# Windowed attention with a gated feed-forward: loads one group less ahead, keys transposed behind x, the third group's weights transposed by DMA

## The chip, the core and the metric

The kernel runs on one core of one Trainium2 chip. The metric is the device time of one execution in microseconds (us). The profile is one execution, taken by the hardware profiler. Engines: PE is TensorE (its weight loads are listed as PEld), DVE VectorE, ACT ScalarE, POOL GpSimd, SP SyncE, which here only issues DMAs. Each engine works through its own instructions in the order in which they are written; an instruction that waits holds up all behind it on that engine. A DMA runs beside the engines once it is issued.

## The reference

Attention with four sink keys and a window of 128, on 4 batches, 8 heads, 768 positions, 64 columns a head; then a feed-forward block on the joined heads.

```python
scores = scale * np.matmul(q, k.transpose(0, 1, 3, 2))
keep = (pos[None, :] < n_sink) | ((rel >= 0) & (rel < window))
a = softmax(np.where(keep, scores, -1e9))
x = np.matmul(a, v)            # then (4 * 768) x 512, heads side by side
h = x @ w_in                   # 512 -> 2048
out = (h * sigmoid(1.702 * h)) @ w_out
```

## The kernel before

The 3072 positions are cut into 12 groups of 256 (`NG`, three to a batch), and a group into two blocks of 128. What happens to a group:

- **Loads** (`load_part`, line 123, issued by POOL, float32 to fp16 on the way): parts 0 and 1 are the queries' two blocks, 2 and 3 the keys', into `qkn`; 4 and 5 are the values', into `vn`. Each is 128 KB as fp16.
- **Transposition of queries and keys** into `qkT`: on PE with a copy by ACT or DVE for groups 0 to 3 (`qk_block`), by one DMA of 512 KB on SP's queue for groups from 4 on (`transposed_qk`, line 169).
- **Sinks** (`sinks`: PE and DVE; `sink_keys` first copies a batch's four sink keys out of `qkT`), **scores** of a head pair `hp` (0 to 3) into a PSUM tile `nat` with two buffers, **maxima** on DVE, **weights** (`weights`, line 255: four exponentials on ACT into `A`).
- **Weights transposed** into `AT` (`weights_transposed`): for groups 0 to 2 on PE into a PSUM bank (line 269) with a copy by ACT (271) or DVE (273), for the later ones by a DMA of 128 KB on SP's queue (line 275).
- **lower** (DVE, line 305) and **upper** (POOL, line 318) cut the two triangles out of `AT`, **values** (PE) multiplies them with `vn`, **normal** (DVE, lines 361 and 362) divides by the sums into `xn`.
- **x_transposed**: `xn` into `xT`, by a DMA of 256 KB on SP's queue for groups from 2 on (line 380).
- **hidden** (PE, line 394, then the gelu on ACT, line 397): eight tiles, `F2` 0 to 7, in two PSUM banks `mm`. **o** (`out_part`, line 409): the second matrix, two blocks of four parts, and `out_store` (a copy by ACT or DVE and a DMA on SP's queue).

The order is written out by hand. Lines 442 to 628 hold the start, in which groups 0 to 2 and the first pieces of the feed-forward are interleaved. Then follows the main loop. **Round n** has these parts for group n's attention, group n-1's hidden phase and group n-2's output:

1. `second(n, ...)`, for n over 2: weights of head pairs 0 and 1 and their transposition, the output matmuls of group n-2 with scores and maxima of pairs 2 and 3 in between, the two stores, weights and transpositions of pairs 2 and 3, `lower(n, 0)`, and at its end `transposed_qk(n + 2)`. In rounds 5 and 8, where group n+1 opens a batch, POOL copies that batch's sink keys first.
2. On POOL: `upper` of pairs 0 and 1, then the query and key loads of group n+3 with `upper` of pairs 2 and 3 between them.
3. The hidden phase: eight tiles of group n-1. At `F2` = 1 come sinks, scores and maxima of group n+1's pairs 0 and 1 (`ahead`) and `lower(n, 1)`; at `F2` = 3, 4, 6 and 7 the values and normalising of group n; `lower(n, 3)` stands ahead of the first normalising. The two value loads of group n+3 are paced by a small POOL copy of what `normal` wrote (`paced_load`).
4. `x_transposed(n)`.

On SP's queue a round is therefore: x of group n-1 (from the round before), AT pairs 0 and 1, a store, AT pair 2, a store, AT pair 3, queries and keys of group n+2.

Buffers: `qkn` 3, `qkT` 4, `A` 4, `AT` 6, `lo` and `up` 4 each, `xT` and `gT` 3.

Of the kernel before, what the change touches and what calls it, by code (L numbers as in the profile page):

```python
# [57 lines left out]
def kernel(  # L58
# [20 lines left out]
    NG = B * NT  # L79
# [31 lines left out]
    def load_part(g: int, part: int):  # L111


        b, t = divmod(g, NT)
        e, i = divmod(part, 2)
        rows = slice(t * TG + i * P, t * TG + (i + 1) * P)
        if part == 0:
            G[g]["qkn"] = work.tile([P, 4, DM], FP16, tag="qkn", bufs=3, name=f"qkn{g}")
        if part < 4:
            dst = G[g]["qkn"][:, part].rearrange("s (h d) -> s h d", h=H)  # L120
        else:
            dst = vn[b][t][:, i, :, 0:D]
        nc.gpsimd.dma_start(dst, (q, k, v)[e][b, :, rows].rearrange("h s d -> s h d"))  # L123

    def load_qk(g: int):
        for part in range(4):
            load_part(g, part)

    def load_v(g: int):
        for part in (4, 5):  # L130
            load_part(g, part)
# [35 lines left out]
    def transposed_qk(g: int):  # L167
        if g >= EARLY:
            nc.sync.dma_start_transpose(qk_tile(g), G[g]["qkn"].rearrange("p a c -> p (a c)"))
# [79 lines left out]
    def weights(g: int, hp: int):  # L249

        nat, bias = G[g]["nat", hp], G[g]["bias"]
        A = work.tile([P, 4, P], FP16, tag="A", bufs=4, name=f"A{g}_{hp}")
        for h in range(2):
            for i in range(2):
                nc.scalar.activation(  # L255
                    out=A[:, 2 * h + i], in_=nat[:, h, i, P:], func=AF.Exp, bias=bias[:, i, hp, h : h + 1],
                    scale=scale,
                )
        G[g]["A", hp] = A

    def weights_transposed(g: int, hp: int):
        A = G[g]["A", hp]
        AT = work.tile([P, 2, 2, P], FP16, tag="AT", bufs=6, name=f"AT{g}_{hp}")
        flat = AT.rearrange("p h i s -> p (h i) s")
        if g < 3:
            bank = av_bank if g == 2 or (g, hp) == (1, 3) else mm_bank
            tp = bank(f"tA{g}_{hp}", (P, 4, P), FP16)
            for a in range(4):
                nc.tensor.transpose(tp[:, a], A[:, a], ident)
            if g == 0 or hp < (2 if g == 2 else 3):  # L270
                nc.scalar.copy(flat, tp)
            else:
                nc.vector.tensor_copy(out=flat, in_=tp)
        else:
            nc.sync.dma_start_transpose(flat, A.rearrange("p a c -> p (a c)"))
        G[g]["AT", hp] = AT
# [10 lines left out]
    def sink_weights(g: int):  # L287
        ts_ = G[g]["ts"]
        As = sinkA[g % 2]
        nc.scalar.activation(out=As[:, 0:64], in_=ts_.rearrange("p a j -> p (a j)"), func=AF.Exp)  # L290
        G[g]["As"] = As
# [19 lines left out]
    def upper(g: int, hp: int):  # L311
        AT, i0 = G[g]["AT", hp], int(g % NT == 0)
        up = work.tile([P, 2, 2, P], FP16, tag="up", bufs=4, name=f"up{g}_{hp}")
        if i0:
            out, in_, rows = up[:, :, 1], AT[:, :, 1], 2
        else:
            out, in_, rows = up.rearrange("p h i s -> p (h i) s"), AT.rearrange("p h i s -> p (h i) s"), 4
        nc.gpsimd.affine_select(  # L318
            out=out, in_=in_, pattern=[[0, rows], [-1, P]], compare_op=ALU.is_gt, fill=zero_reg, base=0,
            channel_multiplier=1,  # L320
        )
        G[g]["up", hp] = up
# [26 lines left out]
    def paced_load(g: int, part: int, n: int, hp: int):  # L349

        if g < NG:
            nc.gpsimd.tensor_copy(out=pace, in_=G[n]["rcp", hp][0:1, 0, 0:1])
            load_part(g, part)
# [12 lines left out]
    def x_transposed(g: int):  # L366
        xT = work.tile([P, 2 * HP, P], FP16, tag="xT", bufs=3, name=f"xT{g}")
        xn = G[g]["xn"].rearrange("p i a h d -> p (i a h d)")
        if g < 2:
            bank = mm_bank if g == 0 else av_bank  # L370
            for i in range(2):
                tp = bank(f"tx{g}_{i}", (P, HP, P), FP16)
                for c in range(HP):
                    nc.tensor.transpose(tp[:, c], xn[:, (HP * i + c) * P : (HP * i + c + 1) * P], ident)
                if g == 0 or i == 0:
                    nc.scalar.copy(xT[:, bass.ts(i, HP)], tp)
                else:
                    nc.vector.tensor_copy(out=xT[:, bass.ts(i, HP)], in_=tp)
        else:
            nc.sync.dma_start_transpose(xT, xn)  # L380
        G[g]["xT"] = xT.rearrange("p (i c) s -> p i c s", i=2)
# [49 lines left out]
    def out_store(g: int, i: int):  # L431
        b, t = divmod(g, NT)
        osb = work.tile([P, DM], FP32, tag="osb", bufs=3, name=f"osb{g}_{i}")
        if i == 0:
            nc.scalar.copy(osb, G[g]["o", i])
        else:
            nc.vector.tensor_copy(out=osb, in_=G[g]["o", i])
        r = b * S + t * TG + i * P
        nc.sync.dma_start(out[r : r + P, :], osb)
# [54 lines left out]
    def o(g: int, i: int, *parts):  # L494
        if 0 <= g < NG:
            for p in parts:
                out_part(g, i, p)
# [75 lines left out]
    load_part(3, 3)  # L573
    load_v(2)
    load_v(3)
    load_qk(4)
    load_v(4)
    hidden(0, 1)
    sink_transposed(1)
    qk_block(2, 0, by_dve)  # L580
# [17 lines left out]

    for hp in (0, 1):
        weights(2, hp)  # L600
    o(0, 0, 0, 1)
    for a in (0, 1):
        qk_block(3, a, by_dve)
    o(0, 0, 2, 3)
    scores(2, 2)
    maxima(2, 2)
    weights_transposed(2, 0)
    upper(2, 0)
    o(0, 1, 0)
    out_store(0, 0)  # L610
    weights_transposed(2, 1)
    upper(2, 1)
    scores(2, 3)
    maxima(2, 3)
# [9 lines left out]
    lower(2, 0)  # L624
    o(0, 1, 3)
    weights(2, 3)
    sink_weights(2)
    out_store(0, 1)

    def second(n: int, g2: int, att: bool):  # L630

        if att and n + 1 < NG and (n + 1) % NT == 0:
            sink_keys((n + 1) // NT, nc.gpsimd.tensor_copy)
        if att:
            for hp in (0, 1):
                weights(n, hp)
                weights_transposed(n, hp)
        o(g2, 0, 0, 1, 2, 3)
        if att:
            scores(n, 2)  # L640
            maxima(n, 2)
        if g2 == NG - 1:
            out_store(g2, 0)
            out_last(g2, 1)
            return
        o(g2, 1, 0)
        if att:
            scores(n, 3)
            maxima(n, 3)
            sink_terms(n)  # L650
        o(g2, 1, 1, 2, 3)
        out_store(g2, 0)
        if att:
            weights(n, 2)
            weights_transposed(n, 2)
        out_store(g2, 1)
        if att:
            weights(n, 3)
            weights_transposed(n, 3)
            sink_weights(n)  # L660
            lower(n, 0)
            if n + 2 < NG:
                transposed_qk(n + 2)

    for n in range(2, NG + LAG2):
        att = n < NG
        g1, g2 = n - LAG1, n - LAG2

        if n > 2:
            second(n, g2, att)  # L670
        else:
            transposed_qk(n + 2)
        if att:
            if n > 2:
                upper(n, 0)
                upper(n, 1)
            for part in range(4):
                if n + 3 < NG:
                    load_part(n + 3, part)
                if n > 2 and part < 2:  # L680
                    upper(n, 2 + part)
        if n in (2, 3, 4):
            sink_columns(n - 1)

        for F2 in range(NF // 2):
            if 0 <= g1 < NG:
                hidden(g1, F2)
            if not att:
                continue
            if n == 2 and F2 == 0:  # L690
                weights_transposed(n, 3)
                upper(n, 3)
            if F2 == 1:
                sink_transposed(n)
                ahead(n + 1, 0)
                lower(n, 1)
                ahead(n + 1, 1)
            if F2 == 2:
                lower(n, 2)
            for hp, at in enumerate((3, 4, 6, 7) if n + 1 < NG else (4, 5, 6, 7)):  # L700
                if F2 == at:
                    values(n, hp)
                    if hp == 0:
                        lower(n, 3)
                    normal(n, hp)
                    if hp in (1, 2):
                        paced_load(n + 3, 3 + hp, n, hp)
        if att:
            x_transposed(n)
            if n + 1 < NG and (n + 1) % NT == 0:  # L710
                sink_values((n + 1) // NT)

# [33 lines left out]
```

## Time and profile before

| | |
|---|---|
| median of three runs | 243.81 us (243.29 to 244.23) |
| the profiled execution | 243.37 us |
| its span | 241.5 us |
| PE busy | 222.7 us, 92% of the span |
| ACT, DVE, POOL busy | 156.1, 146.1, 104.7 us |
| DMA packets' time on POOL's queue (q0), on SP's (q1) | 78.9% and 43.0% of 16 engines' span |
| mean granted clock of PE | 0.998 |

Times within the profile count from the span's start; the rest of the execution's time, 1.9 us, lies around it. "Busy" of PE is modelled, since matmuls overlap each other; a share near 100% in a stretch means that no idle time is seen there, not that PE is at its peak. The time that packets took counts every packet in flight on an engine, so that shares of the queues can add up to more than 100%.

### The profile page before, as it was taken

The page shows a single profiled execution, that of the slowest core. Times are in us where ns is not written, and L with a number is a line of the kernel's source. Part 1 is how long each engine was busy: PE and PEld are TensorE (multiplying, and loading weights), DVE is VectorE, ACT ScalarE, POOL GpSimd, SP SyncE. Part 2 cuts the span into 40 slices and gives each one's busy share as a digit, 9 for nine tenths or more (in the row PEclk, how much of TensorE's full clock was granted, in tenths as well). Part 3 has the DMA queues.
Part 4 walks back from the last instruction along what each step waited for, and adds up shares of the span by engine and source line. Part 5 has one row for each costly group of instructions (what it writes and reads, how often), then busy time and mean ns, then how long its engine had stood idle before and what let it go on. Part 6 is the DMA issues. An engine that isn't in the chain of part 4 may idle for free.

```text
span 241.5 us, 5809 instructions
## 1 busy us (share of the span) xinstructions
PE 222.7 (92%) x2220; PEld 155.7 (64%) x2220; DVE 146.1 (61%) x389; ACT 156.1 (65%) x355; POOL 104.7 (43%) x158
## 2 busy tenths in 40 slices
PE   1656799999999999999999999999999999999994
PEld 0443678569658569478478487486585685684863
DVE  4688856488568378377667575586682893830100
ACT  2268693784866875785786776677668658760531
POOL 8977486847326447354438057058020310310000
PEclk9999999999999999999999999999999999999999
DMA  8999999999999999999999999999982513503102
GB/s 74 151 188 193 177 207 180 154 120 145 127 150 190 138 165 157 112 189 121 124 183 159 153 163 141 173 134 139 129 214 46 151 25 62 148 11 87 46 0 87
DMA packets 130699, 32.07 MB, mean 133 GB/s; under 512 B 123120, under 2 KB 127728, under 8 KB 130672
## 3 DMA queue, kind: packets, MB, share of 16 engines
q0 software_dynamic: 79104, 13.64, 78.9%
q1 hardware_dynamic: 50992, 17.88, 43.0%
q8 instruction: 17, 0.28, 0.5%
q10 hardware_dynamic: 576, 0.20, 0.3%
q14 instruction: 10, 0.08, 0.1%
HBM read 27.50 MB, written 6.29 MB: 140 GB/s over the span
## 4 chain that ended last, share of the span: by engine, by line
PE 63%; DVE 14%; ACT 13%; DMA 5%; issue 3%; POOL 1%; SPq 0%; ACTq 0%; DVEq 0%; POOLq 0%
PE hT L394 28%; PE o L409 22%; ACT A L255 6%; DVE m L240 5%; DVE nat L236 5%; ACT L397 3%; PE nat L224 3%; DMA AT<-A 2%; PE av L344 2%; DMA qkn<-in_k_dram 2%; ACT gT L397 2%; PE av L332 2%; PE av L340 2%; PE o L420 1%; DVE xn L362 1%
## 5 line engine op out<-in xcount | busy, mean ns | idle before, releaser
L394 PE MATMUL hT<-xT,w_in 128*128 128x256 f16 x768 | 95.1, 274 | 1.1 <-ACT gT L397 0.4
L409 PE MATMUL o<-w_out,gT 128*128 128x512 f16 x368 | 85.4, 380 | 0.0
L397 ACT ACTIVATE gT<-hT 128x512 f16<-128x512 f32 x96 | 56.1, 597 | 41.2 <-PE hT L394 40.9
L394 PEld LDWEIGHTS <-w_in 128*128 128x128 f16 x768 | 72.7, 98 | 13.4 <-issue 0.6
L318 POOL TENSOR_SCALAR_AFFINE_SELECT up<-AT 128x512 f16<-128x512 f16 (+1 forms) x48 | 27.8, 585 | 99.1 <-DMA AT<-A 91.7
L255 ACT ACTIVATE A<-nat,bias 128x128 f16<-128x128 f32 x192 | 53.7, 376 | 18.6 <-DVE bias L244 17.1
L409 PEld LDWEIGHTS <-gT 128*128 128x128 f16 x368 | 33.6, 98 | 37.2
L236 DVE COPY_PREDICATED nat<-prev,nat 128x512 f32<-128x512 uint16 x48 | 33.2, 692 | 28.7 <-PE nat L224 19.0
L240 DVE TENSOR_REDUCE m<-nat 128x4 f32<-128x512 f32 x48 | 33.2, 691 | 1.7
L123 POOL DMA_DIRECT2D vn<-in_v_dram x24 | 21.3, 898 | 3.4 <-DMA w_out<-in_moe_w_out_dram 2.3
L123 POOL DMA_DIRECT2D qkn<-in_k_dram x24 | 21.3, 894 | 2.5 <-DMA w_in<-in_moe_w_in_dram 2.0
L123 POOL DMA_DIRECT2D qkn<-in_q_dram x24 | 21.6, 910 | 1.3 <-POOLq L727 0.8
L305 DVE TENSOR_TENSOR lo<-AT,own 128x512 f16<-128x512 f16 (+1 forms) x48 | 18.2, 397 | 5.9 <-DMA AT<-A 5.7
L362 DVE TENSOR_TENSOR xn<-av,rcp 128x256 f16<-128x256 f32 x48 | 20.4, 424 | 1.7
L340 PE MATMUL av<-vn,up 128*128 128x65 f16 x160 | 18.4, 196 | 0.0
L344 PE MATMUL av<-vn,lo 128*128 128x65 f16 x160 | 18.3, 196 | 0.0
L332 PE MATMUL av<-vs,AsT 128*128 128x130 f16 x80 | 16.5, 224 | 0.6 <-DVE xn L362 0.3
L224 PEld LDWEIGHTS <-qkT 64*128 64x128 f16 x352 | 11.8, 100 | 7.7 <-issue 7.0
L224 PE MATMUL nat<-qkT 64*128 64x128 f16 x288 | 16.6, 232 | 0.0
L361 DVE RECIPROCAL rcp<-av 128x4 f32<-128x4 f32 x48 | 8.5, 178 | 12.3 <-PE av L344 12.0
L340 PEld LDWEIGHTS <-up 128*128 128x128 f16 x160 | 14.8, 100 | 1.4 <-POOL up L318 0.5
L397 ACT ACT_TABLE_LOAD x11 | 14.1, 1283 | 0.2
(58 smaller groups left out, 180.3 us busy)
## 6 DMA issues: line engine op xcount, KB each, us to landing
out_dram<-osb SPq DMA_DIRECT2D x23, 256.0 KB
qkn<-in_q_dram POOLq DMA_DIRECT2D x24, 128.0 KB, 5.6
qkn<-in_k_dram POOLq DMA_DIRECT2D x24, 128.0 KB, 5.4
vn<-in_v_dram POOLq DMA_DIRECT2D x24, 128.0 KB, 6.6
w_in<-in_moe_w_in_dram POOLq DMA_DIRECT2D x4, 512.0 KB, 10.4
w_out<-in_moe_w_out_dram POOLq DMA_DIRECT2D x4, 512.0 KB, 11.6
AT<-A SPq DMA_TRANSPOSE x36
xT<-xn SPq DMA_TRANSPOSE x10
```

The costliest lines, as they stand in the source:

```text
L123: nc.gpsimd.dma_start(dst, (q, k, v)[e][b, :, rows].rearrange("h s d -> s h d"))
L224: nc.tensor.matmul(o, qkT[r, 0, i, hp], keys[r], start=True, stop=True)
L236: nc.vector.copy_predicated(out=nat[:, :, :, P:], mask=kinds(take_prev, g % NT), data=nat[:, :, :, 0:P])
L240: nc.vector.tensor_reduce(out=m1.rearrange("p h i -> p (h i)"), in_=nat.rearrange("p h i c -> p (h i) c")[:, :, P:], axis=AX.X, op=ALU.max,)
L255: nc.scalar.activation(out=A[:, 2 * h + i], in_=nat[:, h, i, P:], func=AF.Exp, bias=bias[:, i, hp, h : h + 1], scale=scale,)
L318: nc.gpsimd.affine_select(out=out, in_=in_, pattern=[[0, rows], [-1, P]], compare_op=ALU.is_gt, fill=zero_reg, base=0, channel_multiplier=1,)
L340: nc.tensor.matmul(av[:, i, h], up[:, h, i], vn[b][J // 2][:, J % 2, head], start=False, stop=False)
L344: nc.tensor.matmul(av[:, i, h], own_w[:, h, i], vn[b][t][:, i, head], start=(I == 0), stop=(I == 0 or h == 1))
L362: nc.vector.tensor_tensor(out=G[g]["xn"][:, :, hp], in0=av[:, :, :, 0:D], in1=rcp.to_broadcast((P, 2, 2, D)), op=ALU.mult)
L394: nc.tensor.matmul(hT[:, f], w_in16[:, c, bass.ts(F, P)], xT[:, :, c], start=(c == 0), stop=(c == 3))
L397: nc.scalar.activation(out=G[g]["gT"][:, 2 * F2 : 2 * F2 + 2].rearrange("p f s -> p (f s)"), in_=hT.rearrange("p f i s -> p (f i s)"), fun ...
L409: nc.tensor.matmul(o, gT[:, F, bass.ts(i, P)], w_out16[:, F], start=(F == 0), stop=(F == NF - 1))
```

## The change

- Groups are loaded one round less ahead: the start no longer loads group 4, and round n loads group n+2 instead of n+3, at the same places; so round 9 has loads too.
- `transposed_qk(n + 2)` moves from `second` (for n = 2: from the top of the loop) to the end of the round, behind `x_transposed(n)`. On SP's queue it then stands behind x of group n and ahead of the next round's four AT.
- Group 2's weights are transposed by DMA like the later groups', each right behind its weights; the upper triangle of its fourth pair is issued in the start, ahead of group 4's loads.

```diff
@@ weights_transposed
-        if g < 3:
-            bank = av_bank if g == 2 or (g, hp) == (1, 3) else mm_bank
+        if g < 2:
+            bank = av_bank if (g, hp) == (1, 3) else mm_bank
...
-            if g == 0 or hp < (2 if g == 2 else 3):
+            if g == 0 or hp < 3:
@@ the start
     load_v(2)
     load_v(3)
-    load_qk(4)
-    load_v(4)
...
     for hp in (0, 1):
         weights(2, hp)
+        weights_transposed(2, hp)
     o(0, 0, 0, 1)
...
-    weights_transposed(2, 0)
     upper(2, 0)
     o(0, 1, 0)
     out_store(0, 0)
-    weights_transposed(2, 1)
     upper(2, 1)
...
     weights(2, 3)
+    weights_transposed(2, 3)
     sink_weights(2)
     out_store(0, 1)
+    upper(2, 3)
@@ second
             lower(n, 0)
-            if n + 2 < NG:
-                transposed_qk(n + 2)
@@ the main loop
         if n > 2:
             second(n, g2, att)
-        else:
-            transposed_qk(n + 2)
...
-                if n + 3 < NG:
-                    load_part(n + 3, part)
+                if n + 2 < NG:
+                    load_part(n + 2, part)
...
-            if n == 2 and F2 == 0:
-                weights_transposed(n, 3)
-                upper(n, 3)
...
-                        paced_load(n + 3, 3 + hp, n, hp)
+                        paced_load(n + 2, 3 + hp, n, hp)
         if att:
             x_transposed(n)
+            if n + 2 < NG:
+                transposed_qk(n + 2)
```

## The prediction

> **What bounds the kernel now.** I read the page's busy shares and chain first, then the work by stage, one stage for each round of the main loop, cut where the round's hidden phase starts.
>
> ```profile
> PE 63%; DVE 14%; ACT 13%; DMA 5%; issue 3%; POOL 1%; SPq 0%; ACTq 0%; DVEq 0%; POOLq 0%
> ```
>
> ```profile
> 70.48:87.33 16.85, 16.74 (x166) 11.46 (x165) 10.54 (x29) 12.34 (x30) 7.09 (x13) 1.00 1.41 143
> 87.33:104.62 17.29, 17.21 (x179) 11.93 (x178) 11.08 (x29) 12.31 (x29) 9.43 (x16) 1.00 1.57 162
> 104.62:122.41 17.79, 17.37 (x178) 11.93 (x177) 12.58 (x30) 12.30 (x29) 8.87 (x12) 1.00 1.52 137
> 122.41:139.23 16.82, 16.74 (x166) 11.47 (x165) 10.54 (x29) 12.30 (x29) 7.28 (x13) 1.00 1.53 170
> 190.72:208.37 17.65, 17.21 (x178) 11.94 (x177) 11.80 (x30) 12.67 (x30) 2.55 (x4) 1.00 0.32 76
> ```
>
> After the stretch stand its length and the busy time of PE, PEld, DVE, ACT and POOL. PE is idle only 0.08 to 0.11 us of a round (length less PE's busy time), so TensorE is the bound. In the third of these rows, round 5, it is idle 0.42. The chain of waits says why: round 5's fourth weight transposition.
>
> ```profile
> 105.97 6.02 DMA AT<-A
> ...
> 112.02 0.04 DVE lo L305
> 112.05 0.31 issue
> 112.36 0.18 DVE rcp L361
> ```
>
> That transposition landed 7.37 us after the hidden phase began at 104.62 and cost 0.42 - 0.08 = 0.34 us. In round 8 it landed 6.97 after (the chip's completion count in the trace: 163.49 against 156.52) and cost nothing. So a fourth tile that lands later than about **7.0 us into the hidden phase** holds PE, microsecond for microsecond. Nothing in this kernel has much slack against its DMAs, and it is their order that the change moves.
>
> **Part one, on the path: the third group's weights leave PE.** PE's own rows in time order:
>
> ```profile
> 47.90 0.40 PE L269 MATMUL tA<-ident,A 128*128 128x128 f16 x4
> ...
> 49.00 0.39 PE L269 MATMUL tA<-ident,A 128*128 128x128 f16 x4
> ...
> 52.09 0.38 PE L269 MATMUL tA<-ident,A 128*128 128x128 f16 x4
> 52.31 1.03 PE L409 MATMUL o<-w_out,gT 128*128 128x512 f16 x4
> 53.17 1.04 PE L394 MATMUL hT<-xT,w_in 128*128 128x256 f16 x8
> 54.05 0.39 PE L269 MATMUL tA<-ident,A 128*128 128x128 f16 x4
> ```
>
> From each start to PE's next start: 0.23, 0.32, 0.22 and 0.22 us, with 0.25 of idle time ahead of the third (four output matmuls start at 50.97 and take 0.86). Together 1.24. Not all of it reaches the end: the second hidden tile needs the bank that VectorE empties. That copy runs at 53.38 to 54.07 and, with one AT copy gone before it, can end at 53.48 (the keys' copies end at 52.37, then 0.42 for a lower triangle, 0.69 for the copy). Then 0.87 for the tile and 0.88 for the sinks and scores: the third tile starts at 55.23 instead of 56.03. **Gain 0.8 us.** ScalarE loses two copies (0.58 each), but its chain to the first gelu waits for VectorE's maxima; gain nothing.
>
> In their place stand four DMA transpositions. Alone, one lands 2.4 us after its issue (round 9's and 10's rows). The first is issued when its weights are ready, about 46.9, among loads that fill the DMA until 48.45; VectorE wants it at 52.4. The last is ready about 52.6, lands about 55.1 and is wanted at 59.0. So all are hidden; if the loads held the first for over 5 us, the 0.8 would be gone. [...]
>
> **Part two: loads one group less ahead.** Group 4's six loads leave the start. They were the last there (issued 41.87 to 47.56), nothing else waits behind them, so the start gains nothing. They return in round 2 behind the fourth upper triangle, about 55.8 to 59.4, and land about 63; the transposition of group 4 then comes at 64. No stall there. Each later round loads as many bytes at the same places as before, and round 9, which had none, now loads group 11. But the keys now land just before they are needed.
>
> **Part three: the keys' transposition (qkT) goes from the end of SP's queue of a round to just behind x's.** This is SP's queue around round 5, its start and the time it held the queue:
>
> ```profile
> 97.71 1.23 SPq L380 DMA_TRANSPOSE xT<-xn  x1
> 99.80 2.54 SPq L275 DMA_TRANSPOSE AT<-A  x2
> 102.44 0.52 SPq L439 DMA_DIRECT2D out_dram<-osb  x1
> 103.90 1.19 SPq L275 DMA_TRANSPOSE AT<-A  x1
> 105.54 0.33 SPq L439 DMA_DIRECT2D out_dram<-osb  x1
> 105.97 1.22 SPq L275 DMA_TRANSPOSE AT<-A  x1
> 107.41 3.79 SPq L169 DMA_TRANSPOSE qkT<-qkn  x1
> ```
>
> Let X be x's issue (97.71). The hidden phase starts at X+6.9. Now qkT stands ahead of all four AT:
> - It starts when its last key load has landed: after X by 0.9, 1.7, 2.6, 2.1, 2.0, 2.8 us in rounds 3 to 8 of the trace (completion counts), mean X+2.0; not before X+1.3, when x's issue ends.
> - It holds SP for 3.5 us (mean of the seven issues beside other transfers, 2.86 to 4.01). The one of round 9, after the last load, took 1.77.
> - Two AT, a store, an AT, a store, back to back: 2.54 + 0.52 + 1.19 + 0.33 and gaps = 5.0 us to the fourth AT's issue.
> - That AT lands 4.2 us later (3.8, 3.6, 6.0, 2.6, 5.1, 5.6, 2.6 in rounds 3 to 9). The long ones were issued beside POOL's next load, which will be so in nearly every round, since both now follow the second AT.
>
> Sum: X+14.7, or 7.8 us into the hidden phase; the limit is 7.0. **Stall 0.8 us a round.** It needs a contended round: 4 to 9, six of them, 4.8 us. (Round 3 finds the queue less full; in round 10 no load is left: 2.0 + 3.5 + 5.0 + 2.5 - 6.9 = 6.1, no stall.) Bounds, by the shortest and longest rows: 1.3 + 1.8 + 5.0 + 2.6 - 6.9 = 3.8, no stall; 2.8 + 4.0 + 5.0 + 6.0 - 6.9 = 10.9, 3.9 a round. I take the means.
>
> The first users of qkT itself: the sinks' matmuls 1.9 us into the hidden phase. It lands about X+8.5, against X+8.8: just in time. In rounds 5 and 8 POOL must first copy the sink keys out of it (two copies, 0.44); I put 0.3 us on each, 0.6 together. The first AT then lands near X+9 and VectorE's lower triangle of it slips by up to 0.5, which is inside the 0.6 us between VectorE's normalising of tile 0 and PE's need of its bank (94.69 and 95.25).
>
> What disappears: qkT no longer competes with the key loads, and round 5's old 0.34 is replaced by the new stalls. Sum: -0.8 - 0.35 + 4.8 + 0.6 = **+4.25 us**. The profiled execution took 243.37 us (span 241.5); on it that is 247.6, and on the median of 243.81 it is **248.1**.
>
> **Rivals.**
> *The queue hides it* (not slower). If the qkT issue costs near 1.8 and the fourth AT near 2.6, as in the rows of round 9, every wait ends before 7.0 us and only the gains stay: -0.8, or -1.15 with round 5's stall gone; at best -1.6 if the full 1.24 comes through. 242.2 to 243.0, taken as 242.7. It decides at a sum of X+13.9. For it: this forecast lies only 0.8 beyond that point. Against: the short rows all stand where no load runs. Size against landing, alone: 128 KB 2.4 us, 256 KB 3.04, 512 KB 4.25, so 256 KB more cost 1.2 us, some 215 GB/s. [...] Chance 0.27.
>
> *SP blocked until x's has landed.* In rounds 3 to 9 SP's qkT issue ended from 0.8 us before to 2.5 after the landing of the AT ahead of it, whatever its start, so SP may be held by what is still under way. x's lands 5.3 to 6.7 us after issue, mean 6.1. Then qkT's issue ends at X+6.6, and 6.6 + 5.0 + 4.2 - 6.9 = 8.9: 1.9 us of stall a round, in seven rounds, 13.3, less 1.15: **256.0**. Against it: in rounds 3 to 9 the first AT was issued behind an unfinished x in 1.2 us. Chance 0.22.
>
> *The first part's gain is not there* because the loads hold the four AT: 0.8 more on the forecast, 248.9. Chance 0.05; the forecast itself 0.46.
>
> **How the numbers follow.** About 0.5% (1.2 us) is what a measurement of this kernel can tell from no change. Below 242.6 lies the better part of the first rival's reach only: 0.10. Within 0.5%, to 245.0: the rest of it and a little of the forecast's lower side, where the stall is 0.2 a round: 0.22. Slower: 0.68. For the range I take 242.2, the first rival's best, to 256.0, the second rival's value; above it lie half of that rival and the longest rows, 0.14, below it some 0.03.
>
> **What would show it.** In the profile after: no tA for the third group and the hidden phase of round 2 about 0.8 us earlier; SP's queue in the order x, qkT, AT; the fourth AT landing 7 to 8 us into the hidden phase; POOL's upper triangles, and so the key loads, later by as much; VectorE's lower triangle of the fourth tile waiting for DMA in rounds 4 to 9; rounds of 18.0 us instead of 17.2. A qkT issue near 1.8 us, or rounds of 17.2, would prove me wrong on the good side; PE waiting at the sinks' or scores' matmuls for qkT would show that I took the wrong consumer.

## The result, and the profile after

The changed kernel takes 262.58 us in the median (five runs, 260.85 to 264.77) against 243.81 before: the ratio is 1.076, its 95% interval 1.073 to 1.080. It is slower by 18.8 us, where 4.3 us had been forecast and 256.0 was the upper end of the range. The profiled execution of after took 261.98 us, its span is 260.1 (241.5 before).

The chain of waits on the page of after, by engine:

```profile
PE 51%; DMA 22%; DVE 13%; ACT 5%; SPq 5%; issue 2%; POOL 0%; DVEq 0%; ACTq 0%
```

PE had 63% of the chain and DMA 5%. A fifth of the span is now spent on waiting for transfers, and SP's queue itself appears.

The work by stage in after, cut at the starts of the hidden phases of rounds 4 to 6 and 10; the columns are those of the same view of before:

```profile
87.44:108.29 20.85, 17.48 (x178) 11.82 (x177) 11.10 (x29) 12.30 (x29) 9.60 (x14) 1.00 1.15 137
108.29:127.97 19.68, 17.48 (x179) 11.89 (x178) 12.34 (x30) 12.31 (x29) 9.64 (x14) 1.00 1.15 144
127.97:146.95 18.98, 17.06 (x166) 11.38 (x165) 11.42 (x30) 13.44 (x33) 7.21 (x12) 1.00 1.30 126
...
208.69:225.97 17.28, 17.27 (x177) 11.83 (x178) 10.35 (x28) 11.07 (x24) 4.14 (x6) 1.00 0.52 127
sum 155.99, PE 138.01 PEld 93.44 DVE 90.11 ACT 98.27 POOL 63.83; mean PE 17.25 PEld 11.68 DVE 11.26 ACT 12.28 POOL 7.98
```

The last line sums rounds 3 to 10. The same line of before:

```profile
sum 137.89, PE 136.53 PEld 94.03 DVE 91.44 ACT 98.45 POOL 55.40; mean PE 17.07 PEld 11.75 DVE 11.43 ACT 12.31 POOL 6.92
```

PE's work in a round is as before, but it is idle 3.4, 2.2 and 1.9 us of rounds 4 to 6 (length less PE's busy time). Round 10, behind which no load is left, has no idle time at all. Over rounds 3 to 10 PE was idle 1.4 us before and is idle 18.0 us now; that is 16.6 of the 18.6 us between the two spans. In rounds 3 to 8 the 16 DMA engines were not busier: the DMA column (the last but one) is 1.07 to 1.30 where it was 1.41 to 1.59. Only round 9, which loads now, rose, from 0.54 to 1.32.

SP's queue of after around round 5, as it was shown of before:

```profile
101.39 1.23 SPq L380 DMA_TRANSPOSE xT<-xn  x1
104.61 3.16 SPq L169 DMA_TRANSPOSE qkT<-qkn  x1
107.93 2.54 SPq L275 DMA_TRANSPOSE AT<-A  x2
110.60 0.50 SPq L439 DMA_DIRECT2D out_dram<-osb  x1
111.61 1.20 SPq L275 DMA_TRANSPOSE AT<-A  x1
112.91 0.52 SPq L439 DMA_DIRECT2D out_dram<-osb  x1
113.54 2.22 SPq L275 DMA_TRANSPOSE AT<-A  x1
```

The keys' transposition (qkT) waits from 102.62, where x's issue ends, to 104.61 for its last key load, then holds the queue. The fourth AT is issued 12.2 us after x, where it was 8.3 before. It lands at 117.55 (the completion count), 9.3 us into the hidden phase. What stands behind it, first on DVE, then on PE:

```profile
117.57 0.43 DVE L305 TENSOR_TENSOR lo<-AT,own 128x512 f16<-128x512 f16 x1 [1.42 <-DMA AT<-A]
```

```profile
118.60 0.22 PE L332 MATMUL av<-vs,AsT 128*128 128x130 f16 x1 [1.72 <-DVE xn L362]
```

VectorE sits before the fourth tile's lower triangle until the AT has landed; the first normalising is queued behind it; PE has no free bank for the values of the third head pair until that has run. PE's waits of this kind over the whole run are the first two of these lines (total, times, longest, in us); the other two are its waits for qkT and for what is copied out of it, at the sinks' matmuls:

```profile
PE av L332 <- DVE xn L362: 10.3, 4, 3.4
PE av L344 <- DVE xn L362: 3.4, 3, 2.1
PE sk L195 <- DMA qkT<-qkn: 1.7, 2, 1.2
PE sk L195 <- POOL kd L174: 0.5, 1, 0.5
```

Before, waits for the normalising came to 0.3 us, and there was none at the sinks' matmuls in the rounds.

### The profile page after: what moved, and what is told of

Same layout as the page of the kernel before. It is cut to its first block, busy times and chain, and to the rows that moved or that the text cites. A ratio compares the mean times of both kernels' runs of the same rounds, so it can differ in the third digit from the quotient of the medians.

```text
span 260.1 us, 5788 instructions
## 1 busy us (share of the span) xinstructions
PE 223.2 (86%) x2204; PEld 154.0 (59%) x2204; DVE 145.3 (56%) x387; ACT 155.2 (60%) x353; POOL 106.5 (41%) x160
## 4 chain that ended last, share of the span: by engine, by line
PE 51%; DMA 22%; DVE 13%; ACT 5%; SPq 5%; issue 2%; POOL 0%; DVEq 0%; ACTq 0%
PE o L409 22%; PE hT L394 18%; DMA AT<-A 17%; DVE nat L236 3%; DMA xT<-xn 3%; DVE m L240 3%; PE nat L224 3%; DVE xn L362 2%; ACT A L255 2%; PE av L344 2%; SPq L169 2%; PE av L332 2%; DMA vsr<-in_v_dram 1%; SPq L451 1%; PE o L420 1%
## 5 line engine op out<-in xcount | busy, mean ns | idle before, releaser
L318 POOL TENSOR_SCALAR_AFFINE_SELECT up<-AT 128x512 f16<-128x512 f16 (+1 forms) x48 | 29.4, 614 | 101.9 <-DMA AT<-A 81.0
L255 ACT ACTIVATE A<-nat,bias 128x128 f16<-128x128 f32 x192 | 53.7, 376 | 20.4 <-DVE bias L244 18.8
L332 PE MATMUL av<-vs,AsT 128*128 128x130 f16 x80 | 16.5, 223 | 10.6 <-DVE xn L362 10.3
L123 POOL DMA_DIRECT2D vn<-in_v_dram x24 | 21.3, 896 | 3.5 <-DMA w_out<-in_moe_w_out_dram 3.5
L123 POOL DMA_DIRECT2D qkn<-in_k_dram x24 | 21.3, 895 | 1.5 <-DMA w_in<-in_moe_w_in_dram 1.5
## 6 DMA issues: line engine op xcount, KB each, us to landing
out_dram<-osb SPq DMA_DIRECT2D x23, 256.0 KB
w_out<-in_moe_w_out_dram POOLq DMA_DIRECT2D x4, 512.0 KB, 12.4
```

What stands on the lines that cost most here:

```text
L255: nc.scalar.activation(out=A[:, 2 * h + i], in_=nat[:, h, i, P:], func=AF.Exp, bias=bias[:, i, hp, h : h + 1], scale=scale,)
L318: nc.gpsimd.affine_select(out=out, in_=in_, pattern=[[0, rows], [-1, P]], compare_op=ALU.is_gt, fill=zero_reg, base=0, channel_multiplier=1,)
```

## The experiments

All ratios are against runs of the kernel before on the same chip (243.8 to 244.3 us).

### e1: the weights alone

```diff
 the kernel before, and of the change only:
-        if g < 3:
+        if g < 2:                       # weights_transposed by PE
...
     for hp in (0, 1):
         weights(2, hp)
+        weights_transposed(2, hp)
...
     weights(2, 3)
+    weights_transposed(2, 3)
     sink_weights(2)
     out_store(0, 1)
+    upper(2, 3)
```

> The kernel before with the third group's weights transposed by DMA, and nothing else. My step: 0.8 us less, some 243.0 against 243.8. Rival: the loads that fill the DMA hold these four transpositions, or the queue delays group 4's keys: no gain or 1 us more.

Measured 247.20 us, ratio 1.012 (1.008 to 1.016): 3 us slower. That is the rival's way, and more than the 1 us that it named. DVE's timeline of this run:

```profile
54.84 0.42 DVE L305 TENSOR_TENSOR lo<-AT,own 128x512 f16<-128x512 f16 x1 [2.81 <-DMA AT<-A]
```

The first of the four AT was issued at 46.8 and landed at 54.8, 8 us later, among group 4's loads; in the changed kernel, where these loads are gone, the same transposition lands 2.5 us after its issue. VectorE waits in front of the triangle with the copy behind it that empties PE's bank, so PE stands for 2.8 us. And its clock falls. These are stretches of this run; the clock granted to PE is the third number from the end, 1.00 being full speed:

```profile
53.20:55.90 2.70, 0.00 (x0) 0.00 (x0) 1.03 (x2) 1.21 (x2) 0.93 (x2) 0.94 1.43 155
55.90:59.50 3.60, 3.58 (x38) 2.79 (x38) 1.36 (x5) 0.60 (x1) 3.03 (x7) 0.57 1.04 208
```

2.7 us of idle time, and right behind it 3.4 us at half the clock.

### e7: the weights of pairs 2 and 3 alone

```diff
 e1, and
-        if g < 2:
+        if g < 2 or (g == 2 and hp < 2):     # pairs 0 and 1 on PE, in their old places
```

> The kernel before with only pairs 2 and 3 of the third group's weights transposed by DMA, pairs 0 and 1 on PE as before. If it was the first pairs' transpositions, held by group 4's loads, that made the weights-only kernel slow, these two cost nothing, and the 0.7 us of PE time is gained: 242.5 to 243.5. If the DMA transpositions in the start cost by themselves (loads of group 5 later, queue longer): 245 to 247.

Measured 242.85 us (twelve runs), ratio 0.995 (0.993 to 0.998). That is the gain of part one without its loss, and the one version here that beats both kernels, by 1 us. So the loss of e1 came from the two early transpositions: in e1 VectorE waited 2.8 us for the first, which landed 8 us after its issue among the loads.

### e8: matmuls in the idle time

```diff
 e1, and
                 hidden(g1, F2)
+            if n == 2 and F2 == 0:
+                warm = av_bank("warm", (P, DM))
+                for _ in range(12):
+                    nc.tensor.matmul(warm, ident, w_out16[:, 0], start=True, stop=True)
```

> The weights-only kernel (247.2) with twelve matmuls of 512 columns whose result nobody uses, put on PE where it stood idle for 2.8 us at 53 us. In that profile the granted clock was 0.5 for 3.4 us right behind the idle time. If the idle time lowers the clock, the clock stays at 1.0 there and some 1.7 us come back: 245 to 246. If the clock falls for another reason: 247 or more.

Measured 246.58 us, 0.6 less than e1 and between the two forecasts. The same two stretches in its profile:

```profile
53.20:55.90 2.70, 2.70 (x15) 1.27 (x13) 1.03 (x2) 1.31 (x2) 1.89 (x5) 1.00 0.83 230
55.90:59.50 3.60, 3.60 (x57) 3.21 (x55) 2.58 (x8) 1.29 (x3) 3.60 (x5) 1.00 0.98 194
```

The clock stays at 1.00 and PE does 57 matmuls in the second stretch instead of 38. In the profiled executions the way from the hidden phase of round 2 to that of round 3 shrinks from 21.3 to 19.7 us, the 1.7 expected. The medians do not show it. Each is to be taken against before on its own chip: e1 is 3.0 us behind it and e8 2.8, a difference that lies within the noise. Not every run of e1 loses its clock (the granted mean of its six runs is 0.983 to 0.998), and the profiled e8 lost 0.75 us to a late AT in round 5. So the two profiles fit that the idle time lowers the clock here, but one of each is no proof, since idle times of 3.4 and 3.0 us in after had no drop behind them (last section); how much it is worth in the median stays open.

### e2 and e3: the order alone, and order with loads

```diff
 e2: the kernel before, and              # loads of group n+3 stay
             lower(n, 0)
-            if n + 2 < NG:
-                transposed_qk(n + 2)
...
             x_transposed(n)
+            if n + 2 < NG:
+                transposed_qk(n + 2)
 e3: e2, and the loads of group n+2 (the whole change without the weights)
```

> The kernel before (loads of group n+3 in round n, as before) with the keys' transposition moved behind x's, and nothing else. Theory A, the order on SP's queue costs most and the late keys add to it: the transposition then starts 1.3 us after x's issue instead of 2.7, so some 9 us of the 19 go, 253 to 255. Theory B, the late keys are nearly all of it: 244 to 246. Theory C, the order alone does it and the keys' lateness does not matter: 261 to 263.

> The changed kernel with the third group's weights transposed on PE again (loads and order changed, weights not). If part one gains its 0.8 us in the changed kernel too: 263.4. If the added DMA transpositions are a cost there: under 262.

Measured: e2 260.55 us, ratio 1.069 (1.063 to 1.074); e3 262.76, ratio 1.074 (1.069 to 1.079). The order alone costs 16 us of the 19. The later loads may add some 2, but the intervals of e2 and e3 overlap, and the weights' part changes nothing that these runs can tell (262.58 with, 262.76 without). My theory A fell: in e2 qkT starts 1.4 to 1.9 us after x, so the wait for the keys is gone, and yet the fourth AT lands 7.0 to 11.1 us into the hidden phase in rounds 3 to 9. PE waits before the values, and now longer for qkT itself as well, at the sinks' matmuls:

```profile
PE av L332 <- DVE xn L362: 5.8, 3, 4.1
PE sk L195 <- DMA qkT<-qkn: 5.1, 3, 3.2
PE av L344 <- DVE xn L362: 4.1, 2, 2.1
```

The profiled run of e2, at 263.1 us the longest of its four, also ran 13.7 us of its rounds at half the clock, so part of the 16 us in the medians may be the clock behind the waits.

### e9: one group alone

```diff
 the kernel before, and transposed_qk(7) behind x_transposed(5), all others in their old place
```

> The kernel before, with the keys' transposition of one single group (the eighth) moved behind x's, so that it stands ahead of round 6's four AT. Theory A, each moved transposition costs its own round and nothing else: the order alone cost 16.4 us in seven rounds, so some 1.5 to 3.5 us, 245.3 to 247.3, and rounds 7 to 10 as before. Theory B, the delay feeds itself from round to round through x and the loads: later rounds are longer than before's 16.8 to 17.4 us too, 248 or more. Theory C, one late round is absorbed: within 0.5 us of before.

Measured 247.63 us, ratio 1.015 (1.012 to 1.019). Rounds 5 to 7 of its profile:

```profile
105.40:123.16 17.76, 17.20 (x178) 11.94 (x177) 12.37 (x31) 12.70 (x30) 6.66 (x10) 1.00 1.10 128
123.16:142.33 19.17, 16.90 (x166) 11.46 (x165) 10.72 (x29) 12.30 (x29) 7.25 (x13) 1.00 1.29 154
142.33:159.61 17.28, 17.20 (x178) 11.91 (x177) 12.05 (x29) 12.26 (x29) 9.44 (x16) 1.00 1.31 158
```

Round 6, the only one with the moved transposition, takes 19.17 us; it took 16.82 before. Its fourth AT lands 9.1 us into the hidden phase and PE waits 2.2 us, which is what lies beyond the limit of 7.0. The next round is back at 17.28. So this moved transposition pays in its own round, 2.3 us in the profile; in the median the kernel loses 3.3, which is within theory A's 1.5 to 3.5. If the others cost as much, seven such rounds are 16 to 23 us, an estimate; the order alone cost 16.

### e10: SP held by small loads

```diff
 the kernel before, order unchanged, and
             x_transposed(n)
+            if n < NG - 2:
+                for j in range(8):
+                    nc.sync.dma_start(small[:, j], v[0, :, 4 * j : 4 * j + 4])
```

> The kernel before, order unchanged, with eight small loads (8 KB each, into a tile that nobody reads) issued on SP behind x's transposition in rounds 2 to 9. In the profile of before such a load held SP for some 0.7 us, so together they hold it as long as the keys' transposition with its waits, with almost no bytes. Theory A, the time on SP's queue ahead of the fourth AT is what costs: the fourth AT is issued some 4 us into the hidden phase, 252 to 260. Theory B, the bytes of the transposition on the DMA engines are what costs: 243.5 to 246.

Measured 275.70 us, ratio 1.124 (1.118 to 1.129). SP's queue in it (its line numbers are one higher than before's):

```profile
129.62 5.75 SPq L713 DMA_DIRECT2D small<-in_v_dram  x8
...
135.49 2.51 SPq L276 DMA_TRANSPOSE AT<-A  x2
...
140.70 1.22 SPq L276 DMA_TRANSPOSE AT<-A  x1
```

Eight loads of 8 KB, an eighth of qkT's bytes in all, hold SP for 5.8 us; the fourth AT is issued 12.4 us after x (128.34), as in the changed kernel, and PE stops at the same place, before the values:

```profile
PE av L333 <- DVE xn L363: 14.9, 5, 4.8
PE av L345 <- DVE xn L363: 7.8, 3, 3.4
```

It is slower than the changed kernel and than theory A's 252 to 260. Each load holds SP for 0.7 us, so eight hold it longer than qkT does; and behind five of the waits the granted clock was 0.5, for 20.5 us together in the profiled run (277.3 us), which costs some 10 us of PE's time, an estimate (half of 20.5). Theory A in its mechanism: the time on SP's queue costs, not the bytes.

### e6: the stores off SP's queue

```diff
 the changed kernel, and in out_store
-        nc.sync.dma_start(out[r : r + P, :], osb)
+        eng = nc.gpsimd if 1 <= g <= NG - 3 else nc.sync
+        eng.dma_start(out[r : r + P, :], osb)
```

> The changed kernel with the output stores of the rounds with attention issued by POOL instead of SP (two of them stand between the first and the fourth AT on SP's queue, 1.3 us with their gaps). Theory A, the length of SP's queue from the keys' transposition to the fourth AT sets the round: 1.3 us less in some seven rounds, 252 to 256. Theory B, the DMA engines' work or the loop through the key loads sets it: 260 to 264.

Measured 250.43 us, ratio 1.023 (1.017 to 1.029), somewhat below theory A's 252 to 256. SP's queue around round 5:

```profile
100.90 1.23 SPq L380 DMA_TRANSPOSE xT<-xn  x1
102.78 3.02 SPq L169 DMA_TRANSPOSE qkT<-qkn  x1
105.96 5.42 SPq L275 DMA_TRANSPOSE AT<-A  x4
```

The four AT now follow each other; the fourth lands 5.4 to 7.4 us into the hidden phase in rounds 4 to 10, and the waits before the values shrink from 13.7 to 1.7 us in all, while those for qkT at the sinks' matmuls grow to 4.3. With the same transfers, 12 us come back after two short instructions were taken out of SP's queue. Not all of it is the queue's own length. In rounds 4 to 9 the fourth AT lands 3.3 us sooner after x in the mean: 0.7 us of that lies between qkT and the fourth AT's issue, 1.9 is a quicker landing of that AT, and 0.8 an earlier start of qkT (its hold is 0.1 longer). The key loads, which stand behind the fourth upper triangle, come earlier too, and qkT starts 1.6 to 2.6 us after x. As POOL now issues the stores ahead of its triangles and loads, this run moves those as well; it does not tell the two apart.

### e5: the loads out of the fourth AT's way

```diff
 e2, and the round's four query and key loads behind all four upper triangles
-                upper(n, 0)
-                upper(n, 1)
+                for hp in range(4):
+                    upper(n, hp)
             for part in range(4):
                 if n + 3 < NG:
                     load_part(n + 3, part)
-                if n > 2 and part < 2:
-                    upper(n, 2 + part)
```

> The order-only kernel (260.6) with the round's four query and key loads issued behind all four upper triangles instead of between them. Theory A: the fourth AT lands 4.2 to 6.7 us after its issue because POOL's next load runs beside it; without that it lands after some 2.6, 2 us earlier, and most of the stalls go: 248 to 252. Theory B: SP's queue alone is too long, and the later loads only collide with x's and the keys' transposition instead: 258 to 262.

Measured 260.71 us, ratio 1.068 (1.062 to 1.073): theory B in time, though A's mechanism was there. The fourth AT lands 2.4 to 4.3 us after its issue instead of 2.4 to 6.7, and no wait before the values is left. But the loads, moved later, now run beside qkT, which lands 11.7 to 13.2 us after x in every other round. The largest waits of PE at the sinks' matmuls (total, times, longest):

```profile
PE sk L195 <- DMA qkT<-qkn: 7.2, 2, 4.3
PE sk L195 <- POOL kd L174: 3.3, 1, 3.3
```

And the granted clock falls behind each of them (mean 0.92, 0.85 and 0.85 in rounds 4, 6 and 8). Rounds 5 to 7:

```profile
108.96:126.50 17.54, 17.36 (x178) 11.92 (x177) 12.39 (x30) 12.31 (x29) 8.93 (x14) 1.00 1.22 115
126.50:150.01 23.51, 19.17 (x167) 12.76 (x165) 10.75 (x29) 12.33 (x29) 7.22 (x12) 0.85 1.29 142
150.01:167.59 17.58, 17.37 (x178) 11.84 (x177) 12.01 (x30) 12.61 (x30) 8.21 (x12) 1.00 1.15 114
```

Round 6 is idle 4.3 us and runs at a mean clock of 0.85, 3.5 us more (0.15 of 23.5); rounds 5 and 7 lose only 0.2 us each.

### e4: the lower triangle later

```diff
 the changed kernel, and
                     values(n, hp)
-                    if hp == 0:
-                        lower(n, 3)
...
+                    if hp == 3:
+                        lower(n, 3)
                     values(n, hp)
```

> The changed kernel with VectorE's lower triangle of the fourth tile moved from ahead of the first normalising to ahead of the fourth values. If what PE waits for is VectorE blocked behind that triangle, the limit moves from 7.0 us to some 8.9 us into the hidden phase and some 1 us a round comes back: 254 to 257. If PE waits for POOL's upper triangles or the loop through the key loads closes all the same: 260 to 263.

Measured 262.38 us, ratio 1.071 (1.065 to 1.078): nothing came back. PE no longer waits for the normalising, so x comes earlier against the fourth AT, and then SP waits for the keys. SP's wait for key loads (total, times, longest), first in after, then in e4:

```profile
SPq L169 <- DMA qkn<-in_k_dram: 8.8, 7, 1.8
```

```profile
SPq L169 <- DMA qkn<-in_k_dram: 21.7, 10, 4.3
```

PE's waits moved, most of them to the sinks' matmuls (10.3 us instead of 2.2), and some to POOL's upper triangles:

```profile
PE sk L195 <- DMA qkT<-qkn: 9.0, 5, 2.2
PE av L340 <- POOL up L318: 4.5, 5, 1.9
```

This fits a loop that is longer than a round of PE's work: fourth AT, upper triangle, key loads, qkT, next round's fourth AT. Where PE waits in it is then secondary. The loop is argued from these rows. It is no condition of the loss: in e2 the keys are loaded a group earlier, so qkT does not wait for them, and the kernel takes 260.55 us all the same.

## Why the prediction was wrong

**The bound, right.** TensorE bounds the kernel; a fourth AT beyond 7.0 us holds it. In rounds 4 to 6 of after it lands 10.4, 9.3 and 7.8 us in, and PE waits 2.2 (after 1.2 for qkT), 1.7 (after 0.5) and 0.8 us. One reading beside it was too smooth: the prediction gives PE's idle time as 0.08 to 0.11 us a round, but its fifth row, round 10, shows 0.44; there PE waited for ScalarE's gelu, and nothing in the forecast hangs on it.

**Part one, near in size, and dependent on part two.** The hidden phase of round 2 starts 0.64 us earlier in after, and its third tile, for which the forecast was 0.8, starts 0.5 us earlier (55.53 against 56.03). e7, where the two last pairs alone change, gains 1.0 in the median. That the loads could hold the four AT was a rival at 0.05 and 0.8 us; e1 shows that where the loads stay it turns the gain into a loss of 3 us. In the changed kernel group 4's loads are gone from the start. The prediction says so under part two, but still counts on loads under part one; it did not see that the first part needs the second.

**Part two, mostly right.** No stall in round 2, nothing gained in the start. Its late keys cost perhaps 2 us (e3 against e2, not clear of the noise), and in e4 most of PE's waiting is for what they delay.

**Part three, wrong, at the sum X+14.7.** Rounds 4 to 9 of after, in the prediction's terms (us):

| term | forecast | measured |
|---|---|---|
| qkT starts after x | 2.0 | 2.7 |
| it holds SP | 3.5 | 3.5 |
| to the fourth AT's issue | 5.0 | 5.6 |
| to its landing | 4.2 | 4.8 |
| into the hidden phase (less 6.9; in one round, less 8.0) | 7.8 | 9.6 |

The step that failed is the sum X+14.7, made by "I take the means": it came out near X+16.6. Three of its four terms were 0.6 to 0.7 us too short, and the sum is compared with a limit, so 0.8 us beyond it became 2.6. Waits before the values came to 13.7 us where 4.8 were forecast, at the sinks' matmuls to 2.2 instead of 0.6, and for x's transposition to 1.8, where none was forecast. The first term has a cause that the bullet list missed: the key loads are issued behind the fourth upper triangle, so a late AT makes the next round's keys late. The prediction names this among its signs ("and so the key loads, later by as much") but keeps 2.0 in the sum. In e6, with the fourth AT earlier, the term is 1.9; in e4, where x no longer waits for that AT, it is 4.1. The term of 5.0 was short by itself: back to back, with stores of 0.53 us each and the gaps between, the shortest of the six rounds took 5.4. For the landing, e5 shows that the loads beside it matter: without them it is 2.4 to 4.3 us, with them 2.4 to 6.7 (e2).

**The range missed too**, by 6.6 us, and its top was one rival's value, not the longest rows: those gave 3.9 us a round, more than the 2.6 measured. In the profiled run, 262.0 us, the waits alone explain it: it has no drop of the clock in the rounds (1.00 in each), and PE's idle time there grew by 16.6 us where the top of the range left 12.2. The clock comes on top in other runs: the mean granted clock of the five is 0.974 to 0.991, and each 0.01 is some 2.6 us, an estimate (0.01 of 260).

**The rivals.** That the queue hides it fell. *SP blocked until x's has landed* came nearer in number than the forecast (13.3 us of stalls and 256.0; 13.7 us measured before the values), but not as it was stated: in rounds 7, 8 and 10 of after SP's qkT issue ended 0.8, 0.5 and 2.1 us before x landed. The means lie close all the same, the issue's end at X+6.2 and x's landing at X+5.9 in rounds 4 to 9, so that SP is held longer while x is in flight is not excluded; no run tries it. The stalls are longer because qkT started later and what stood behind it took longer, while its own hold came out as forecast.

**What stays open.** How much of the medians is the clock: e8 changed it in one place only. Why some idle times lower it and others do not (last section). How much of e6's gain is SP's queue and how much the moved loads.

## What to carry to other kernels

What the transposition cost here was the time for which it holds the issuing engine (3.5 us in the mean), paid by all that is queued behind it; look at what the last transfer of the queue releases, and by when, before anything is put in front of it. Where forecast times meet a deadline, add the terms at their late values too: here an excess of 0.8 us tripled when three of four terms slipped by 0.6 to 0.7 us. A stall of PE can cost more than itself: with 15 of 26 idle times of 2.0 us or more the granted clock dropped to 0.5 here (next section).

## What the runs showed of the hardware

- Behind PE's idle time of 2.8 us in e1 the granted clock was 0.5 for 3.4 us; in e5, round 6, it was 0.5 for 6.8 us, from 2.7 us into an idle time of 4.3. Idle times of 2.0 us (e10, at 122.9) and 2.1 (e3, at 137.4) had such a drop too; those of 3.4 and 3.0 us in rounds 7 and 8 of after, and one of 3.4 in e10 (at 79.2), had none. From 45 us on, all twelve traces together show 26 idle times of 2.0 us or more before their last 6 us: 15 had a drop, which began before their end or at most 1.7 us behind it, and 11 had none. No drop there stands without such an idle time. The length of the idle time alone does not tell the two kinds apart: 2.0 us had a drop, and 3.4 us had none.
- SP is held 0.7 us by a load of 8 KB (e10), 1.2 us by most transpositions of 128 or 256 KB (up to 2.4 for one of 128 KB in after), and by one of 512 KB for 1.4 us in round 10 of e5, behind the last load, and 2.8 to 5.2 us in its rounds 3 to 9.
- A transposition of 128 KB landed 2.4 us after its issue in round 10 of before and of after, where no load is left, and 8 us after it among 128 KB loads issued by POOL (e1).
